# A new instruction order from planned times, and six more spinning products in the opening

## The chip, the cores and the metric

The kernel runs on one core of one Trainium2 chip. The metric is device time in microseconds (us) for one execution of the whole program. Beside the timed runs there is one execution under the hardware profiler, and all the lines quoted come from that one. The engines are TensorE (PE, with its weight loads shown as PEld), VectorE (DVE), ScalarE (ACT), GpSimd (POOL) and SyncE (SP). Each runs its own instructions in order, and they wait for each other through semaphores.

## What is computed

A sequence of 2048 rows of 512 passes twice through a pair of blocks, A and B, each added to its input after a layer norm.

```python
def _A_ref(x, mem0, Wq, Wk, Wv, Wo, seg_len):        # 32 heads of 128, 8 memory rows, segments of 32
    for s in range(n_seg):
        xs = x[:, s * seg_len:(s + 1) * seg_len, :].copy()
        h = jnp.concatenate([mem, xs], axis=1)
        q, k, v = (einsum('btd,dhe->bhte', h, W) for W in (Wq, Wk, Wv))
        scores = jnp.where(mask, einsum('bhqe,bhke->bhqk', q, k) * scale, -1e9)
        o = einsum('bhqk,bhke->bhqe', softmax(scores), v)
        o = einsum('bhte,hed->btd', o, Wo)
        mem = o[:, :M, :].copy()
        outs.append(o[:, M:, :])
...
x = x + _A_ref(_layernorm(x), A_mem0, A_Wq, A_Wk, A_Wv, A_Wo, A_seg_len)
x = x + _B_ref(_layernorm(x), B_wqkv, B_wo)          # linear attention, 32 heads of 16
x = x + _A_ref(_layernorm(x), A_mem0, A_Wq, A_Wk, A_Wv, A_Wo, A_seg_len)
x = x + _B_ref(_layernorm(x), B_wqkv, B_wo)
```

What matters is the loop in A: 64 segments a layer, and the first eight rows of a segment's output are the memory rows that the next segment begins with. So the segments form one long chain, and everything else has to be fitted around it.

## The kernel before

All of Wq, Wk, Wv and Wo lie in SBUF (16 MB, loaded once in the opening, 1 MB or half a MB at a time). A segment's 40 columns (8 memory rows, 32 rows of x) are handled in two parts: the memory rows with the first 24 rows of each segment go through the segment's own steps, while the last 8 rows of four segments are gathered into a "left" block of 32, which is projected ahead of time. The eight heads of a quarter sit in four column strips of the PE array, so nearly every product is a group of four matmuls with 32 columns of weights each, side by side. A product over 512 inputs is four such groups, one a quarter of the weight matrix (c = 0 to 3), summed in one of eight PSUM banks.

One segment of the chain, by the names of its nodes and the lines of its matmuls:

- `kq0`, `kq1`: key and query products of the two halves of the heads (L2282, and L2139 where the weights are already loaded), copied out (L2009 on ACT or L2010 on DVE) and transposed on DVE (L2301);
- `v`: value products;
- `mem0`, `mem1`: for each half the scores (L2434 and L2426), their exponentials (L2441, L2445), a mask (L2449) and the product with the values for the memory rows (L2462), then a reciprocal, a scaling and a transpose (L2467 to L2469);
- `out`: eight groups of the output product (L2554), copied out;
- `next`: the new memory rows, turned into columns by two small products (L2584) and copied into the next segment's block;
- `x`: attention of the other rows (L2504, L2524), which nothing in the chain waits for;
- `left0`, `left1`, `leftv`, `prep`, `res`, `bi`, `bo`, `bl`: left blocks, layer norms, residuals, and the steps of block B, which are woven in.

No loop sets the order. Each operation is a node with a key (layer, step, name) and a count within it. A table, `PLACE`, holds one number for each node; `schedule` sorts all nodes by it, and each engine issues its own in that order. A letter behind the number chooses the engine of a copy that either can do: `a` for ACT, `v` for DVE. Another table, `BANKS`, gives the PSUM bank of each product. In this version the numbers are ranks, of 13,822 nodes:

```python
    (0, 39, "next"): "4257 4258 4262a",
    (0, 40, "kq0"): "4265 4269 4271 4273 4281a 4289 4277a 4285",
```

`finalize` turns the dependencies into semaphore waits. Where a node has more than one, all but the one expected last may be moved to an earlier instruction of the same engine that waits for nothing, if the producer is expected to be done by then. The expectation is made of ranks: the producer's rank plus 60 for a DMA, or plus 2 and 9 times its cost.

In the opening the weights arrive over the queue of SP: four quarters of Wk, four of Wq, four of Wv, eight pieces of Wo. PE meanwhile projects the keys and queries of left blocks 0 to 6 (`sk` and `sq`, two halves each), those of blocks 3 to 6 being written to HBM (`spill`, on POOL, after the last piece of Wo) and read back later (`lre`, on SP). Before there is anything to do, PE "spins": `spin` multiplies a tile of ones by itself, three groups of four 256-column matmuls for each spin (L2167). There are eight spins, and every first key or query product is ordered behind the last of them.

## Time and profile before

| | us |
|---|---|
| median of three runs | 1471.38 |
| lowest and highest | 1468.09, 1471.46 |
| the profiled execution | 1467.64 |
| its span, first to last instruction | 1465.6 |

The profile's page gives busy time by engine, the chain of waits that ended last, and groups of instructions by line. In a group's row stand the output and input, the shape, the count, the busy time, the mean length of one in ns, and the idle time of the engine just before with what ended it. In a timeline's row stand the start and the length in us, then engine, line and operation; an "x" counts instructions merged into the row. Lengths of matmuls include the pipeline's drain, so two rows can overlap; the distance between two starts tells how fast PE really goes. The granted clock of the profile is 1.00 throughout.

### The profile page before, as it was taken

Reading aid. Unit: us, or ns where it says so; the run is one execution under the profiler, and the core shown is the slowest. Engines: PE = TensorE matmul, PEld = TensorE weight load, DVE = VectorE, ACT = ScalarE, POOL = GpSimd, SP = SyncE. Lnnn points to the kernel's source line nnn. Section 1 sums busy time; section 2 is a strip of 40 time slices with the busy share of each in tenths; the row PEclk is TensorE's granted clock in tenths of the full one; section 3 lists DMA queues with packets and bytes.
Section 4 is the critical chain, followed back from the end, with each engine's and each line's share of the span. In section 5 each row is a group of like instructions: output and inputs, shape, how many; then the busy total and the mean of one; then the engine's idle time right before and its main releaser. Section 6 shows DMA issues by size and latency. Waiting matters only on the chain.

```text
span 1465.6 us, 90842 instructions
## 1 busy us (share of the span) xinstructions
PE 1440.9 (98%) x43565; PEld 830.5 (57%) x39581; DVE 1222.8 (83%) x3879; ACT 922.6 (63%) x2620; POOL 205.4 (14%) x407
## 2 busy tenths in 40 slices
PE   8999999999999999999999999999999999999998
PEld 4455655655555555555455555556565555655555
DVE  4788888888888888988888888888788888888878
ACT  4656566666656666565566666656766766666657
POOL 3111111011111101111201110111111011111010
PEclk9999999999999999999999999999999999999999
DMA  9421111111011011002300101111001011101034
GB/s 386 151 72 43 18 51 37 31 22 29 22 21 21 19 24 25 25 22 46 75 21 21 26 21 28 25 27 28 22 22 28 24 29 25 29 18 25 28 65 129
DMA packets 84967, 65.12 MB, mean 44 GB/s; under 512 B 65544, under 2 KB 76360, under 8 KB 83048
## 3 DMA queue, kind: packets, MB, share of 16 engines
q1 hardware_dynamic: 70584, 40.21, 10.4%
q0 software_dynamic: 13840, 18.98, 4.5%
q8 instruction: 325, 5.32, 1.5%
q14 instruction: 58, 0.48, 0.1%
q10 hardware_dynamic: 160, 0.14, 0.0%
HBM read 27.80 MB, written 14.02 MB: 29 GB/s over the span
## 4 chain that ended last, share of the span: by engine, by line
PE 93%; DVE 4%; DMA 2%; ACT 1%; issue 1%; SPq 0%; DVEq 0%
PE pb L2282 43%; PE pb L2554 19%; PE pb L2139 14%; PE pb L2504 3%; PE pb L2151 3%; PE pb L2741 2%; PE pb L2462 2%; PE pb L2524 2%; PE pb L2426 2%; PE pb L2584 1%; DMA Wk_sb<-in_A_Wk_dram 1%; DVE arena_sb L2010 1%; PE pb L2434 1%; DVE arena_sb L2301 0%; DMA arena_sb<-xn_scratch 0%
## 5 line engine op out<-in xcount | busy, mean ns | idle before, releaser
L2009 ACT ACTIVATE arena_sb<-pb 128x512 bf16<-128x512 f32 (+3 forms) x1036 | 515.1, 527 | 245.8 <-PE pb L2139 107.7
L2282 PE MATMUL pb<-Wk_sb,arena_sb 128*32 128x512 bf16 x4320 | 357.3, 382 | 3.8 <-DMA Wk_sb<-in_A_Wk_dram 1.5
L2282 PE MATMUL pb<-Wv_sb,arena_sb 128*32 128x512 bf16 x4608 | 328.7, 378 | 0.0
L2554 PE MATMUL pb<-Wo_sb,arena_sb 128*32 128x256 bf16 x10368 | 322.7, 273 | 3.3 <-issue 2.4
L2301 DVE STREAM_TRANSPOSE arena_sb<-arena_sb 128x256 f32<-128x256 f32 x640 | 259.5, 425 | 38.4 <-ACT arena_sb L2009 31.2
L2554 PEld LDWEIGHTS pb<-Wo_sb,arena_sb 128*32 128x32 bf16 x10368 | 265.9, 97 | 40.3 <-DVE arena_sb L2469 8.7
L2026 POOL DMA_DIRECT2D dx_sb<-y_sb x246 | 125.5, 514 | 1008.0 <-DVE y_sb L2566 369.8
L2282 PE MATMUL pb<-Wq_sb,arena_sb 128*32 128x512 bf16 x3088 | 235.4, 379 | 0.1
L2282 PEld LDWEIGHTS pb<-Wk_sb,arena_sb 128*32 128x32 bf16 x4320 | 117.4, 97 | 193.9 <-issue 91.1
L2477 ACT ACTIVATE arena_sb<-pb,arena_sb 128x128 bf16<-128x128 f32 x539 | 163.5, 368 | 66.7 <-DVE arena_sb L2511 33.5
L2139 PE MATMUL pb<-Wq_sb,arena_sb 128*32 128x512 bf16 x2032 | 199.4, 379 | 0.0
L2479 DVE TENSOR_TENSOR arena_sb<-pb,arena_sb 128x128 bf16<-128x128 f32 (+2 forms) x391 | 157.1, 402 | 9.0
L2282 PEld LDWEIGHTS pb<-Wv_sb,arena_sb 128*32 128x32 bf16 x4608 | 113.1, 96 | 80.5 <-issue 8.5
L2010 DVE CAST arena_sb<-pb 128x512 bf16<-128x512 f32 (+2 forms) x226 | 112.0, 500 | 40.6 <-PE pb L2139 12.2
L2009 ACT ACTIVATE outW_sb<-pb 128x256 f32<-128x256 f32 (+1 forms) x132 | 50.5, 383 | 139.0 <-PE pb L2554 90.5
L2282 PEld LDWEIGHTS pb<-Wq_sb,arena_sb 128*32 128x32 bf16 x3088 | 82.9, 97 | 87.8 <-issue 21.2
L2514 DVE STREAM_TRANSPOSE arena_sb<-arena_sb 128x192 f32<-128x192 f32 x256 | 93.5, 365 | 19.3 <-ACT arena_sb L2477 16.7
L2492 DVE TENSOR_TENSOR arena_sb<-arena_sb,wx_sb 128x1280 bf16<-128x1280 bf16 x128 | 102.0, 797 | 1.8 <-ACT arena_sb L2445 1.1
L2504 PE MATMUL pb<-arena_sb 128*32 128x130 bf16 x3072 | 102.4, 220 | 0.9 <-issue 0.8
L2449 DVE TENSOR_TENSOR arena_sb<-arena_sb 128x256 bf16<-128x256 bf16 x252 | 70.1, 280 | 22.5 <-ACT arena_sb L2441 19.5
L2504 PEld LDWEIGHTS pb<-arena_sb 128*32 128x32 bf16 x3072 | 67.7, 96 | 30.3 <-issue 9.2
L2566 DVE TENSOR_TENSOR y_sb<-pb,outW_sb 64x256 bf16<-64x256 f32 x162 | 68.7, 424 | 16.4 <-ACT outW_sb L2009 11.1
(135 smaller groups left out, 1793.9 us busy)
## 6 DMA issues: line engine op xcount, KB each, us to landing
Wk_sb<-in_A_Wk_dram SPq DMA_DIRECT2D x4, 1024.0 KB, 10.7
Wq_sb<-in_A_Wq_dram SPq DMA_DIRECT2D x4, 1024.0 KB, 17.4
Wv_sb<-in_A_Wv_dram SPq DMA_DIRECT2D x4, 1024.0 KB, 25.3
Wo_sb<-in_A_Wo_dram SPq DMA_DIRECT2D x8, 512.0 KB, 22.1
xs_scratch<-x_sb POOLq DMA_DIRECT2D x32, 128.0 KB, 2.5
pq_scratch<-arena_sb POOLq DMA_DIRECT2D x23, 128.0 KB, 2.6
xn_scratch<-arena_sb POOLq DMA_DIRECT2D x20, 128.0 KB, 2.8
lk_scratch<-arena_sb POOLq DMA_DIRECT2D x8, 256.0 KB, 4.1
```

The source lines that it names most:

```text
L2009: return e.activation(o() if callable(o) else o, i() if callable(i) else i, ACTF.Copy)
L2010: return e.tensor_copy(o() if callable(o) else o, i() if callable(i) else i)
L2026: add(eng, lambda e: e.dma_start(o, i), 0.55 if eng == "pool" else 0.66, reads=reads, writes=writes, dsem="%s%d" % (kind, k), lat=lat + (0 ...
L2139: return pe.add_instruction(mybir.InstMatmult(name=nc.get_next_instruction_name(), engine=mybir.EngineType.PE, ins=[pe.lower_ap(x), pe.low ...
L2282: r = pe.matmul(o, blk[:, c, :], w, start=(c == 0), stop=(c == 3), tile_position=(0, 32 * j))
L2301: add("dve", lambda v: v.transpose(dst, src(img[:, k, :].bitcast(F32))), 0.445, reads=[("img", k, h) for h in range(2)], writes=[dkey])
L2477: x = e.activation(o[:, u, :], i()[:, u, :], ACTF.Copy, scale=r[:, u:u + 1])
L2479: return e.tensor_tensor(o, i(), r.unsqueeze(2).to_broadcast([128, n, 128]), ALU.mult)
L2492: add("dve", lambda v: v.tensor_tensor(Px.rearrange("p b (n j x) -> p b n j x", n=20, j=4), PQx[:, r2].rearrange("p b (n x) -> p b n x", n ...
L2504: r = pe.matmul(pv.f32()[32 * i:32 * i + 32, 130 * k:130 * k + 130], cols(b, k, i), vimg[:, r2, 4 * b + i, :], start=True, stop=True, skip ...
L2514: add("dve", lambda v, b=b, k0=k0: v.transpose(oTb[:, s1, b, :, :, k0:k0 + 3].rearrange("p h j k q e -> p k (h j) (q e)").bitcast(F32), ox ...
L2554: r = pe.matmul(tl.f32()[32 * j:32 * j + 32, 0:256], oT[:, b, f, n, :, :, e], Wo_sb[:, 16 * b + 4 * n + 2 * f + e, 256 * d:256 * d + 256], ...
```

## The change

The table `PLACE` is replaced as a whole, and so is `BANKS`. The nodes and their keys are the same apart from nine more spins. The new numbers are planned times in ns instead of ranks. The same two lines, with those they are read with in the prediction, old and then new:

```diff
-    (0, 39, "next"): "4257 4258 4262a",
-    (0, 39, "x"): "4242 4251 4252 4256 4266 4268v 4283 4294 4295 4296 4304 4313v 4331 4253 4254 4263 4279v 4302",
-    (0, 40, "kq0"): "4265 4269 4271 4273 4281a 4289 4277a 4285",
-    (0, 42, "left1"): "4231 4235 4249 4259 4272v 4275 4333a 4342",
+    (0, 39, "next"): "444451 444529 444870a",
+    (0, 39, "x"): "442488 443680 443850 444607 445022 445225v 445810 443736 443793 444664 446090 446283v 450524 443906 449926 450271 450452a 451109",
+    (0, 40, "kq0"): "445152 445584 446016 446448 447202v 447920 447111a 448260",
+    (0, 42, "left1"): "444020 444721 450935 451367 455086v 455805 456272a 456901",
```

The opening's spins, first products and reads, old and then new:

```diff
-    (0, -3, "spin"): "13 17 18 21 24 28 46 65",
-    (0, 0, "kq0"): "61 79 119 124 229 233 234 240 239a 244 276a 282",
-    (0, 4, "sk"): "82 83 108 122 129a 133",
+    (0, -3, "spin"): "2904 3232 3559 3886 4214 4542 6201 6529 7614 7942 8713",
+    (0, -2, "spin"): "10719 11046 11374 11701 12029 12356",
+    (0, 0, "kq0"): "9208 17551 18198 20898 35788 36004 37299 37515 37222a 37861 38813a 40853",
+    (0, 4, "sk"): "9640 14414 16903 19596 20255a 20885",
```

The expectation in `finalize` is now the producer's planned time, plus its latency and 200 ns for a DMA, or its cost and 100 ns (300 on PE):

```diff
-        place = {nd: i for i, nd in enumerate(self.committed)}
         source = {}
         for nd in self.committed:
             if nd.dsem is not None:
-                source[sidx[nd.dsem], nd.dval] = place[nd] + 60
+                source[sidx[nd.dsem], nd.dval] = nd.t + 1000 * nd.lat + 200
             elif nd.sig:
-                source[sidx[nd.eng], nd.val] = place[nd] + 2 + 9 * nd.cost[nd.eng]
+                source[sidx[nd.eng], nd.val] = nd.t + 1000 * nd.cost[nd.eng] + (300 if nd.eng == "pe" else 100)
...
-                        if source[w] >= place[o]:
+                        if source[w] > o.t:
```

The opening has eleven spins instead of eight ahead of the first products, and six more behind the products of the first quarter of Wk: `lead` holds the first groups of blocks 0 and 2 (both halves) and of 4 and 5 (one half). With the first group of `kq0`, which `hold` puts ahead of the six as well, these make seven groups. The other three groups of `kq0`'s key product and of all the others come behind the last of the six:

```diff
-            last = spin(0, -3, "spin", 8, fresh=3)
+            last = spin(0, -3, "spin", 11, fresh=3)
             early[0] = True
+            lead, rest = [], []
...
-                        for n in P.nodes[n0:]:
-                            if n.engs == ("pe",):
-                                n.order.update(last)
+                        mine = [n for n in P.nodes[n0:] if n.engs == ("pe",)]
+                        mine[0].order.update(last)
+                        if not u and G in (0, 2, 4, 5) and not (G > 2 and b):
+                            lead.append(mine[0])
+                        rest += mine[1:]
+            n0 = len(P.nodes)
+            last = spin(0, -2, "spin", 6, after=lead)
+            for n in rest:
+                n.order.update(last)
+            hold.extend([P.nodes[n0], last[0]])
...
+                    if not b:
+                        hold[0].order.add(P.nodes[n0])
+                        for n in P.nodes[n0 + 1:n0 + 4]:
+                            n.order.add(hold[1])
```

The reads of spilled keys and queries have four semaphores instead of two:

```diff
-                        writes=[(nm, G % 2, b) for b in range(2)], dsem="dlr%d" % u, lat=3.5)
+                        writes=[(nm, G % 2, b) for b in range(2)], dsem="dlr%d" % (2 * (G % 2) + u), lat=3.5)
```

More of the change, by code (lines that the diff above doesn't have):

```diff
@@ L1598 @@
[L1598 to L1602 removed]
+    "5012300000002233403606556732127530265702617371111110143430427612101762547164571615674120565271153721"
@@ new lines @@
+    "5327354723537241374215432547015731472453172531512433701572432472670637427362432136472317243172363045"
+    "4105473612764724356123442516212556106712760122162601673210732076750551362765170231701234057641206421"
+    "0675432132431024715647542657121434012762512471564716457213645162560211307026107260270651240736420635"
+    "1600274206537043601604325160532405320457752354730052053725012730123746023017546374015214052714625071"
+    "2521732746630215602657037061307314073176010570410735106472064672650134524365421425537621056324523436"
@@ L1603 @@
+    "0047054136572140704125760034163231666357511357301273063046275163520761247501753067257435745703417504"
+    "3146635461316224254650036601253360146213402536154221042763415724015273174603763037703626421453412531"
+    "5137061046310463075065741765703540613460514726437141475731744322145273270766611046523023710461420054"
+    "4233422775401633735115"
 )
@@ L2305, in a_layer @@
         early = [False]
+        hold = []
         def lroom(G):
@@ L2688, in a_layer @@
                 if b or first and s == 0:
+                    n0 = len(P.nodes)
                     tk, tq = [project(blk, bk, p)[0] for p in parts]
+                    if not b:
+                        hold[0].order.add(P.nodes[n0])
+                        for n in P.nodes[n0 + 1:n0 + 4]:
+                            n.order.add(hold[1])
                 else:
```

40 lines of the change are left out of this document (15 added, 25 removed), and 3100 rows, old and new, of the table PLACE.

## The prediction

> **What bounds the kernel now.** I read the page's head and its chain of waits first, then the busy times by stage, then the timeline of the stretches where TensorE (PE) is not full, and last the two tables of the diff, node by node.
>
> ```profile
> span 1465.6 us, 90842 instructions
> PE 1440.9 (98%) x43565; PEld 830.5 (57%) x39581; DVE 1222.8 (83%) x3879; ACT 922.6 (63%) x2620; POOL 205.4 (14%) x407
> PE 93%; DVE 4%; DMA 2%; ACT 1%; issue 1%; SPq 0%; DVEq 0%
> ```
> ```profile
> 100.00:650.00 550.00, 547.62 (x16886) 319.00 (x15292) 467.96 (x1541) 343.30 (x1008) 77.39 (x148) 1.00 0.12 28
> 650.00:750.00 100.00, 94.23 (x2687) 50.83 (x2456) 83.84 (x250) 56.89 (x150) 18.31 (x33) 1.00 0.23 53
> 750.00:1400.00 650.00, 647.75 (x19956) 374.68 (x17968) 549.85 (x1756) 427.04 (x1232) 85.05 (x163) 1.00 0.10 24
> 1400.00:1466.00 66.00, 58.14 (x1688) 35.57 (x1616) 54.01 (x133) 43.19 (x93) 3.20 (x6) 0.99 0.43 104
> ```
> PE sets the end: 93% of the chain, 98% busy. The columns of the second fence are the stretch, PE, weight loads, DVE, ACT, POOL, clock, DMA. No other engine is full, and no stage is bound by DMA after the opening. But "busy" hides something. A matmul's record ends after its drain, so the records overlap, and a pause of about 0.1 us between two of them shows as no idle time at all. Here is one place in the first layer and one in the second:
>
> ```profile
> 452.31 0.23 PE L2504 MATMUL pb<-arena_sb 128*32 128x130 bf16 x4
> 452.36 0.29 PE L2584 MATMUL pb<-selm_sb,outW_sb 128*32 128x16 f32 x16
> 452.48 0.39 PE L2282 MATMUL pb<-Wq_sb,arena_sb 128*32 128x512 bf16 x4
> 452.70 0.39 PE L2139 MATMUL pb<-Wk_sb,arena_sb 128*32 128x512 bf16 x4
> 453.02 0.40 PE L2282 MATMUL pb<-Wk_sb,arena_sb 128*32 128x512 bf16 x4
> ```
> ```profile
> 1339.48 0.28 PE L2584 MATMUL pb<-selm_sb,outW_sb 128*32 128x16 f32 x16
> 1339.60 0.60 PE L2151 MATMUL pb<-arena_sb 128*32 128x512 bf16 x8
> 1339.89 0.19 DVE L2010 CAST arena_sb<-pb 128x32 bf16<-128x32 f32 x1 [0.16 <-PE pb L2584]
> 1340.14 0.40 PE L2282 MATMUL pb<-Wk_sb,arena_sb 128*32 128x512 bf16 x4
> ```
> Read starts, not lengths. L2584 makes the next memory rows; they are copied out (L2010 here), and only then can the next segment's key and query product (L2282) begin. In between PE has one filler: two groups of four 512-column matmuls, each 0.22 us after the other (452.48 to 452.70). The second group is issued by 452.92, yet the next product starts at 453.02. In the other place 1339.60 + 0.43 = 1340.03, and the product starts at 1340.14. From the last L2584 to the product the hand-over needs about 0.54 us, and the filler covers 0.43. So 0.1 us is lost, unseen in the idle column.
>
> I did this for every PE node: start to start, less the lower quartile of that step among nodes of the same shape. These undisturbed steps add up to 1392.6 us for the whole program, so no order can win more than 1465.6 - 1392.6 = 73 us. Of that, 49 us lie between 100 and 1400 us. By hand-over, over the whole program:
>
> - memory rows to the first product of the next segment: 14.7 us, over 126 hand-overs of which 107 pause (the two places above are of these);
> - second half's scores to its memory product (L2426 to L2462): 5.7 us; first half's: 3.5 us;
> - output product to memory rows (L2554 to L2584): 4.4 us; first memory product to output product (L2462 to L2554): 4.0 us;
> - products to scores, and the second memory product to the output product: 1.7 us together.
>
> **The change part by part.** *The new table.* All operations stay; only their order on each engine changes, and the engine of some copies. A gain can come only from more work standing in these hand-overs. In both tables I added the undisturbed steps of the PE nodes that stand between the two ends, and took the need from the hand-overs that pause now. The shortfall is need less cover, summed.
>
> *Memory rows to next product.* Segment 39 of layer 0 is the place at 452 us. Its old ranks put one filler after "next" (left1, 4259, before kq0 at 4265). The new times put two L2504 groups (x, 444607 and 444664), then left1 (444721), then kq0 (445152). An L2504 group before "next" costs 0.05 us (452.31 to 452.36), 0.056 as quartile, so the cover goes from 0.43 to 0.54. Over all 126 the mean cover goes from 0.43 to 0.52 us; covers under 0.52 fall from 111 to 43. With needs of 0.543 (copy on ACT) and 0.538 (on DVE) the shortfall falls from 15.5 to 5.9. Scaled to the measured 14.7 that leaves 5.6: **-9.1 us**. The groups put there stood elsewhere, so the other hand-overs must be counted too.
>
> *Scores to memory product.* First half: mean cover 1.40 to 1.53 us, shortfall at a need of 1.17 from 5.6 to 0.9, so 3.5 becomes 0.6: **-2.9**. Second half: 1.27 to 1.31, at 1.28 from 14.2 to 11.5, so 5.7 becomes 4.6: **-1.1**.
>
> *Given back.* First memory product to output: 1.31 to 1.25, at 1.13 from 8.5 to 10.6: **+1.0**. Output to memory rows: 0.70 to 0.68, at 0.66 from 3.8 to 4.5: **+0.8**. Second memory product to output: **+0.1**. Second half's products to scores: 1.61 to 1.52: **+0.4**. First half's products to scores: 2.39 to 2.17 us, the largest cut. Only two of these pause today (need about 2.0), and the quickest takes 1.51, so the shortfall grows by 0.3 us (need 1.5) to 4.9 (need 2.0). I take 1.8, a need that lies between: **+1.8**.
>
> *Copies.* 404 move from ACT to DVE and 355 back. DVE gets 49 more:
>
> ```profile
> L2010 DVE CAST arena_sb<-pb 128x512 bf16<-128x512 f32 (+2 forms) x226 | 112.0, 500 | 40.6 <-PE pb L2139 12.2 <-PE pb L2584 8.3 <-PE pb L2504 8.1
> L2009 ACT ACTIVATE arena_sb<-pb 128x512 bf16<-128x512 f32 (+3 forms) x1036 | 515.1, 527 | 245.8 <-PE pb L2139 107.7 <-PE pb L2282 44.9 <-PE pb L2584 31.1
> ```
> At 500 ns, 49 copies bring DVE from 1222.8 to about 1247 us, 85% of the span. Its idle time shrinks by a tenth, and if the pauses left in the middle (about 39 us) grew alike, it would cost 4 us. They wait on other engines too: I take **+1.0**, bounds 0 and 4.
>
> *The opening.*
>
> ```profile
> 2.16 4.03 PE L2167 MATMUL pb<-one_sb 128*32 128x256 bf16 x72 [2.16 <-POOL one_sb L2083]
> 7.44 0.62 PE L2207 MATMUL pb<-id_sb,arena_sb 128*32 128x128 bf16 x16 [0.51 <-DVE arena_sb L2196]
> 7.84 0.86 PE L2167 MATMUL pb<-one_sb 128*32 128x256 bf16 x12
> 9.22 0.62 PE L2282 MATMUL pb<-Wk_sb,arena_sb 128*32 128x512 bf16 x4
> 9.62 0.86 PE L2167 MATMUL pb<-one_sb 128*32 128x256 bf16 x12
> 12.00 0.62 PE L2282 MATMUL pb<-Wk_sb,arena_sb 128*32 128x512 bf16 x4 [1.52 <-DMA Wk_sb<-in_A_Wk_dram]
> ```
> ```profile
> 12.00:14.80 2.80, 2.80 (x28) 1.11 (x32) 0.80 (x3) 0.00 (x0) 2.26 (x8) 1.00 1.00 424
> 14.80:16.90 2.10, 2.10 (x44) 1.03 (x40) 0.00 (x0) 0.00 (x0) 1.59 (x7) 1.00 1.02 429
> ```
> Today PE does one first-quarter product at 9.22, one spin, and waits for the second quarter of Wk until 12.00. It then runs at half speed: 28 matmuls, or 7 groups, in 2.80 us, against 0.22 us a group from 14.8 on. By 16.9 some 18 groups are done. A spin is three groups of four 256-column matmuls, 4.03/6 or some 0.65 us at half speed and 0.33 at full. The new order puts three more spins ahead of the first product, then seven first-quarter products, then six spins, and only then the second quarter. If the three close the hole before 7.44 and the clock has risen by about 9.5, the seven end near 11, the spins near 13, and by 16.9 all 24 groups are done that eight PSUM banks allow with three quarters landed: six groups, 1.3 us ahead. If the clock rises only at 14.8 as today, the first product slips to 10.6 (three spins of 0.65 less the 0.51 idle), the seven end at 13.6, the spins at 16.2, and by 16.9 only 10 groups are done: eight, 1.7 us, behind. The wait that six spins add holds all PE work behind them; nothing else on PE is ready meanwhile, apart from what the second quarter frees at 12.0.
>
> [...]
>
> What is won early meets the last piece of Wo:
>
> ```profile
> L2045 SPq DMA_DIRECT2D Wo_sb<-in_A_Wo_dram x8: 439/2130/6250, 12.1 to 29.7; - x8
> DMA to landing us min/median/max: 18.1/22.1/26.0
> 47.73 1.93 PE L2554 MATMUL pb<-Wo_sb,arena_sb 128*32 128x256 bf16 x64 [0.18 <-DVE arena_sb L2469]
> 48.99 3.76 POOL L2363 DMA_DIRECT2D lk_scratch<-arena_sb  x7 [32.23 <-DMA Wo_sb<-in_A_Wo_dram]
> ```
> It is issued at 29.7 and lands no earlier than 47.8 (shortest flight 18.1) and no later than 48.99, when POOL, which waited for it, goes on. The first output's seventh product, which reads it, comes at 47.73 + 6 x 0.22 = 49.05. So at most 1.25 us and at least 0.06 of a lead survive. I take **-0.5**; bounds -1.25 and +1.7.
>
> *The rest.* The rule that moves a second wait to an earlier instruction now goes by planned times. It changes where an engine stops, not when the producer ends: 0, bounds -1 and +1. The reloads of spilled keys get four semaphores for two; they land many microseconds early: 0. Layer switch and end (650 to 750 and past 1400) lose 5.8 and 7.9 us of PE today; both are reordered, and their waits are on chains of DVE and ACT that stay: 0, bounds -4 and +3.
>
> Sum: -9.1 - 2.9 - 1.1 + 1.0 + 0.8 + 0.1 + 0.4 + 1.8 + 1.0 - 0.5 = -8.5 us. The profiled execution took 1467.6 (span 1465.6 and 2.0 around it), so its like would take 1459.1. The median of the runs, 1471.4, lies 3.7 higher; from it the forecast is **1462.9 us**.
>
> **The rivals.** *The pauses only move.* If a segment is bound by its chain rather than by PE work, cover put into one hand-over is missed in the next: 1471, no change. For it: the same groups are moved. Against it: PE pauses some 49 us over 1300, so per segment it is almost all work, and most hand-overs on the chain do not pause.
>
> *Slower: products to scores.* The one place where the order takes away 0.22 us of cover is L2282 to the first scores (L2434), on a path of two copies and two DVE transposes. If the fuller DVE lifts its need from below 1.9 to 2.5, the shortfall grows by 17.0 us in place of my 1.8: 1462.9 + 15.2 = 1478. At a need of 2.3 (12.2 us) the time is 1473, so it decides from there. Against it: with covers of 1.89 today almost none pauses.
>
> *The clock opens no earlier than today* and six spins at half speed stand in the way: +1.7 for -0.5, so 1465.1; it doesn't change the sign.
>
> *More comes out of it.* The layer switch and the end win their 4 us, and the second half's scores win what the first do (5.7 to 1 us, 3.6 more): 1455.
>
> **How the numbers follow.** A measurement tells about 0.3% (4.4 us) from no change: faster is below 1467.0, slower above 1475.8. Forecast, with its own scatter of 5 us, 0.55; more 0.14; late clock 0.05; pauses only move 0.17; slower 0.09. Of the forecast and the late clock some 0.05 fall within 0.3%, and of the moved pauses 0.05 fall outside, 0.03 of them faster: faster 0.72, same 0.17, slower 0.11. The range 1455 to 1474 holds the forecast, the case of more, and no change.
>
> **What would show it.** In the new timeline two L2504 groups stand between L2584 and L2282 and the product starts right after its filler, with no 0.1 us hole; the 126 pauses add to about 6 us. The first scores start within 0.05 us after the matmul ahead of them. In the opening the seven groups end before 11.5 and 512-column groups go at 0.22 us from 13 on; the first output product waits for Wo. I am wrong if these holes stay, or if L2434 or L2462 opens new ones of 0.1 us in most segments.

## The result, and the profile after

The changed kernel takes 1475.11 us (median of 11 runs, 1471.41 to 1479.71), the kernel before in the same series 1469.98 (11 runs, 1467.17 to 1472.04). The ratio is 1.0036, with an interval of 1.0022 to 1.0050: slower, though by little, where 1462.9 us and a range of 1455 to 1474 were forecast.

The first lines of the page of the changed kernel, and its chain of waits:

```profile
span 1472.8 us, 90913 instructions
...
PE 1434.8 (97%) x43673; PEld 839.5 (57%) x39641; DVE 1244.9 (85%) x3928; ACT 897.7 (61%) x2532; POOL 205.6 (14%) x407
...
PE 86%; DVE 5%; DMA 5%; ACT 1%; SPq 1%; issue 1%; POOL 1%; DVEq 0%
PE pb L2282 39%; PE pb L2563 18%; PE pb L2139 13%; PE pb L2151 3%; PE pb L2513 3%; DMA dx_sb<-y_sb 2%; PE pb L2755 2%; PE pb L2471 2%; PE pb L2533 2%; PE pb L2435 2%; PE pb L2593 1%; DMA arena_sb<-arena_sb 1%; DVE arena_sb L2488 1%; DMA x_s
```

PE fell from 93% of the chain to 86%, DMA rose from 2% to 5%, and a transfer that takes 3.0 us of the chain in the kernel before takes 36.5 us of it here, 2.5% of the span: `dx_sb<-y_sb`. These are the eight small transfers of a residual (L2026, `res`, counts 12 to 19), which bring a block's output rows into the layout of x, four each from the queues of SP and POOL. Only the residual's add (L2633 before, L2642 after) uses them.

The stages of the changed kernel, with the columns of the prediction's second fence (the last 6.8 us of the span are left out):

```profile
100.00:650.00 550.00, 538.23 (x16680) 315.59 (x15108) 467.31 (x1522) 333.28 (x976) 75.28 (x144) 0.99 0.12 26
650.00:750.00 100.00, 94.80 (x2748) 53.39 (x2532) 84.39 (x249) 61.41 (x161) 19.34 (x35) 1.00 0.24 54
750.00:1400.00 650.00, 644.71 (x19904) 380.08 (x17912) 561.53 (x1792) 406.24 (x1162) 83.00 (x159) 1.00 0.10 25
1400.00:1466.00 66.00, 59.50 (x1788) 35.10 (x1708) 56.56 (x144) 45.38 (x104) 6.27 (x12) 1.00 0.38 88
```

In the first layer PE now has 11.8 us without work where it had 2.4, in the second 5.3 where it had 2.3. So this time the loss shows as idle time. What PE and DVE waited for says where. First DVE's waits for the residual's transfers, in us, times and longest, in the kernel before:

```profile
DVE x_sb L2633 <- DMA dx_sb<-y_sb: 3.2, 2, 2.3
DVE arena_sb L2531 <- DMA dx_sb<-y_sb: 0.8, 1, 0.8
```

The same view of the changed kernel, its six costliest rows:

```profile
DVE arena_sb L2523 <- DMA dx_sb<-y_sb: 5.6, 4, 2.8
DVE arena_sb L2010 <- DMA dx_sb<-y_sb: 3.6, 4, 2.4
DVE arena_sb L2842 <- DMA dx_sb<-y_sb: 2.7, 2, 1.7
DVE arena_sb L2301 <- DMA dx_sb<-y_sb: 2.4, 2, 1.4
DVE x_sb L2642 <- DMA dx_sb<-y_sb: 1.8, 1, 1.8
DVE arena_sb L2488 <- DMA dx_sb<-y_sb: 1.7, 1, 1.7
```

17.8 us in 14 stops (20.0 in 17 with two smaller rows), for 4.0 in 3. L2523 and L2301 are transposes, L2010 a copy, L2488 a product, L2842 a step of block B: none of these five reads `dx_sb`. The waits were put on them by `finalize`. And PE's waits in the changed kernel, the two costliest rows:

```profile
PE pb L2443 <- DVE arena_sb L2301: 8.5, 5, 2.4
PE pb L2471 <- DVE arena_sb L2458: 4.8, 3, 1.7
```

They are the first scores behind the transposes, and the memory product behind the mask: the chain, behind a DVE that stands still. The same two rows of the kernel before:

```profile
PE pb L2434 <- DVE arena_sb L2301: 0.5, 1, 0.5
PE pb L2462 <- DVE arena_sb L2449: 0.2, 1, 0.2
```

One place of the first layer shows it whole (timeline of the changed kernel; some rows left out):

```profile
213.65 1.00 POOL L2026 DMA_DIRECT2D dx_sb<-y_sb  x2
...
213.91 0.43 DVE L2301 STREAM_TRANSPOSE arena_sb<-arena_sb 128x256 f32<-128x256 f32 x1
213.93 1.41 SPq L2026 DMA_DIRECT2D dx_sb<-y_sb  x2
...
216.76 0.23 DVE L2010 COPY arena_sb<-arena_sb 128x256 bf16<-128x256 bf16 x1 [2.42 <-DMA dx_sb<-y_sb]
216.90 0.76 DVE L2301 STREAM_TRANSPOSE arena_sb<-arena_sb 128x256 f32<-128x256 f32 x2
...
217.40 0.21 PE L2443 MATMUL pb<-arena_sb 128*32 128x64 bf16 x4 [2.01 <-DVE arena_sb L2301]
```

The copy at 216.76 belongs to a left block (`ql` of segment 17). It carries the wait for the four transfers of SP for the residual of step 16, and DVE, ready for it at 213.91 + 0.43 = 214.34, stood for 2.42 us. The transposes of the keys behind it waited too, and with them PE. The add that needs the data runs at 222.30, 5.5 us later.

Why was the wait put there? One semaphore counts the four transfers, 16 for each, and the program numbers them as it makes the nodes: counts 13, 15, 17 and 19 get 208, 224, 240 and 256. `finalize` takes the planned time of the one that bears the number waited for, 256: 209.919 us, with 2.0 of latency and the 200 ns 212.119, ahead of the copy's 212.310. But the plan issues that transfer first. The one numbered 208 is planned last, at 212.799, and 256 is reached only when all four have landed, by the plan's own times at 214.8, 2.49 us behind the copy. SP's row in the same trace:

```profile
211.87 3.47 SPq L2026 DMA_DIRECT2D dx_sb<-y_sb  x5
```

These five are the four and another small transfer of `res` (count 1), which stands fourth; the starts in the trace are 211.87, 212.58, 213.26, 213.93 and 214.71. The wait ended 2.05 us after the last of them: the plan's latency is right, its transfer is the wrong one. So counted, 13 of the changed kernel's 226 moved DMA waits stand up to 2.5 us ahead of their planned landing, 15.7 us in sum. In the kernel before the same mistake stands in the code, but 60 ranks, some 6.4 us (1465.6 us by 13,822 nodes, times 60), cover the spread of the four; in the change 2.2 us do not.

Nothing behind the copy ran on DVE in the 2.42 us, though the transposes' inputs had no part in the wait.

What the prediction looked for is there too. The hand-over from segment 39 to 40, in the changed kernel:

```profile
455.00 0.29 PE L2593 MATMUL pb<-selm_sb,outW_sb 128*32 128x16 f32 x16
455.12 0.29 PE L2513 MATMUL pb<-arena_sb 128*32 128x130 bf16 x8
455.24 0.40 PE L2282 MATMUL pb<-Wq_sb,arena_sb 128*32 128x512 bf16 x4
455.45 0.40 PE L2139 MATMUL pb<-Wk_sb,arena_sb 128*32 128x512 bf16 x4
455.67 0.40 PE L2282 MATMUL pb<-Wk_sb,arena_sb 128*32 128x512 bf16 x4
455.88 0.40 PE L2139 MATMUL pb<-Wq_sb,arena_sb 128*32 128x512 bf16 x4
```

Two L2513 groups (the old L2504) and a left block's filler stand before the key product, and it starts at 455.67, 0.22 us behind the filler's last group: no hole. It happens at 455.67 instead of 453.02, though.

### The profile page after: what moved, and what is told of

Its sections match the earlier page's. It is cut to its first block, busy times and chain, and to the rows that moved or that the text cites. A ratio compares the mean times of both kernels' runs of the same rounds, so it can differ in the third digit from the quotient of the medians.

```text
span 1472.8 us, 90913 instructions
## 1 busy us (share of the span) xinstructions
PE 1434.8 (97%) x43673; PEld 839.5 (57%) x39641; DVE 1244.9 (85%) x3928; ACT 897.7 (61%) x2532; POOL 205.6 (14%) x407
## 3 DMA queue, kind: packets, MB, share of 16 engines
q1 hardware_dynamic: 70584, 40.21, 10.2%
q8 instruction: 326, 5.34, 1.6%
## 4 chain that ended last, share of the span: by engine, by line
PE 86%; DVE 5%; DMA 5%; ACT 1%; SPq 1%; issue 1%; POOL 1%; DVEq 0%
PE pb L2282 39%; PE pb L2563 18%; PE pb L2139 13%; PE pb L2151 3%; PE pb L2513 3%; DMA dx_sb<-y_sb 2%; PE pb L2755 2%; PE pb L2471 2%; PE pb L2533 2%; PE pb L2435 2%; PE pb L2593 1%; DMA arena_sb<-arena_sb 1%; DVE arena_sb L2488 1%; DMA x_sb<-in_A_x_dram 1%; SPq L2026 1%
## 5 line engine op out<-in xcount | busy, mean ns | idle before, releaser
L2009 ACT ACTIVATE arena_sb<-pb 128x512 bf16<-128x512 f32 (+3 forms) x1013 | 501.4, 524 | 257.5 <-PE pb L2139 108.2
L2282 PE MATMUL pb<-Wv_sb,arena_sb 128*32 128x512 bf16 x4608 | 332.6, 380 | 0.0
L2301 DVE STREAM_TRANSPOSE arena_sb<-arena_sb 128x256 f32<-128x256 f32 x640 | 259.7, 427 | 35.4 <-ACT arena_sb L2009 25.7
L2026 POOL DMA_DIRECT2D dx_sb<-y_sb x246 | 125.2, 513 | 997.6 <-DVE y_sb L2575 459.3
L2282 PE MATMUL pb<-Wq_sb,arena_sb 128*32 128x512 bf16 x3088 | 238.0, 380 | 1.1 <-DVE arena_sb L2010 1.1
L2282 PEld LDWEIGHTS pb<-Wk_sb,arena_sb 128*32 128x32 bf16 x4320 | 122.8, 96 | 176.0 <-issue 87.4
L2139 PE MATMUL pb<-Wq_sb,arena_sb 128*32 128x512 bf16 x2032 | 201.4, 379 | 0.0
L2486 ACT ACTIVATE arena_sb<-pb,arena_sb 128x128 bf16<-128x128 f32 x469 | 142.9, 369 | 72.5 <-DVE arena_sb L2540 22.7
L2488 DVE TENSOR_TENSOR arena_sb<-pb,arena_sb 128x128 bf16<-128x128 f32 (+2 forms) x422 | 171.3, 406 | 11.5 <-DMA dx_sb<-y_sb 1.7
L2010 DVE CAST arena_sb<-pb 128x512 bf16<-128x512 f32 (+2 forms) x248 | 127.4, 516 | 30.9 <-PE pb L2282 8.3
L2282 PEld LDWEIGHTS pb<-Wq_sb,arena_sb 128*32 128x32 bf16 x3088 | 86.0, 97 | 88.1 <-issue 26.3
L2513 PE MATMUL pb<-arena_sb 128*32 128x130 bf16 x3072 | 106.7, 219 | 0.2
L2523 DVE STREAM_TRANSPOSE arena_sb<-arena_sb 128x192 f32<-128x192 f32 x256 | 93.4, 365 | 15.1 <-ACT arena_sb L2486 6.6
L2471 PEld LDWEIGHTS pb<-arena_sb 128*32 128x32 bf16 x2016 | 45.5, 96 | 72.0 <-ACT arena_sb L2009 33.9
L2513 PEld LDWEIGHTS pb<-arena_sb 128*32 128x32 bf16 x3072 | 69.2, 96 | 29.8 <-issue 6.5
```

The source lines that it names most:

```text
L2009: return e.activation(o() if callable(o) else o, i() if callable(i) else i, ACTF.Copy)
L2010: return e.tensor_copy(o() if callable(o) else o, i() if callable(i) else i)
L2026: add(eng, lambda e: e.dma_start(o, i), 0.55 if eng == "pool" else 0.66, reads=reads, writes=writes, dsem="%s%d" % (kind, k), lat=lat + (0 ...
L2139: return pe.add_instruction(mybir.InstMatmult(name=nc.get_next_instruction_name(), engine=mybir.EngineType.PE, ins=[pe.lower_ap(x), pe.low ...
L2282: r = pe.matmul(o, blk[:, c, :], w, start=(c == 0), stop=(c == 3), tile_position=(0, 32 * j))
L2301: add("dve", lambda v: v.transpose(dst, src(img[:, k, :].bitcast(F32))), 0.445, reads=[("img", k, h) for h in range(2)], writes=[dkey])
```

## The experiments

All are compared with the kernel before, run on the same chip in the same series: 1469.42 us for the first four, 1469.51 for the next four, 1467.32 for the three after, 1469.57 for the run after these, 1470.74 for the last two. Ratios have their interval in brackets. "Moved" counts the DMA waits that DVE holds on an instruction other than the one that needs them, from the kernel's own lists; "closest" is the planned time from the transfer to the nearest of them.

**The old expectation on the new order.** The changed kernel, but `finalize` counts in ranks as before:

```diff
-                source[sidx[nd.dsem], nd.dval] = nd.t + 1000 * nd.lat + 200
+                source[sidx[nd.dsem], nd.dval] = place[nd] + 60
...
-                        if source[w] > o.t:
+                        if source[w] >= place[o]:
```

(and the engines' expectation likewise).

> The changed kernel's order, with the old rule for moving a second wait (producer's rank plus 60 for a DMA). Theory A, the moved DMA waits: DVE stops for dx_sb DMAs fall from 20 us to about 4, and the time to 1459 to 1465, faster than before. Theory B, the new order or the fuller DVE is itself slower: the time stays at 1472 to 1478.

1454.53 us, 0.9895 [0.9882, 0.9907]: 149 moved, none closer than 4.9 us. The time lies below theory A's range (1459 to 1465). So the new order, with its engines, banks, opening and four semaphores, wins some 15 us under the old rule, and the new rule takes away some 20. DVE's waits for the transfers fall to the residual's own:

```profile
DVE x_sb L2643 <- DMA dx_sb<-y_sb: 1.7, 3, 0.6
```

**Early waits on the old order.** The kernel before with 25 ranks for a DMA instead of 60:

```diff
-                source[sidx[nd.dsem], nd.dval] = place[nd] + 60
+                source[sidx[nd.dsem], nd.dval] = place[nd] + 25
```

> The kernel before, with one number changed: a DMA is expected 25 ranks after its issue instead of 60 (25 ranks at 106 ns are 2.65 us, what the new rule takes). Theory A: more DMA waits are moved ahead on DVE, its stops for dx_sb DMAs grow from 4 us to 12 or more, and the time is 4 to 15 us above before. Theory B: within 2 us of before.

1480.97 us, 1.0082 [1.0068, 1.0097]: 219 moved instead of 129, the nearest 26 nodes behind its transfer instead of 61. Its costliest rows:

```profile
DVE arena_sb L2010 <- DMA dx_sb<-y_sb: 3.1, 3, 1.6
DVE arena_sb L2514 <- DMA dx_sb<-y_sb: 3.1, 4, 1.0
DVE x_sb L2633 <- DMA dx_sb<-y_sb: 2.5, 3, 1.2
DVE arena_sb L2727 <- DMA dx_sb<-y_sb: 2.4, 1, 2.4
```

The same stops, at the same kinds of instruction, without anything of the new order: 11.6 us.

**No wait moved**, and **a later landing**. Two edits of the changed kernel, each alone:

```diff
-                if e in ("sp", "pool") or nd.key[:2] < (0, 0):
-                    continue
+                continue
```
```diff
-                source[sidx[nd.dsem], nd.dval] = nd.t + 1000 * nd.lat + 200
+                source[sidx[nd.dsem], nd.dval] = nd.t + 1000 * nd.lat + 4200
```

> The changed kernel with no wait moved at all: every wait stays with the instruction that needs it. Theory A: no DVE stop of over 1 us for dx_sb except at the residual's own addition, and 1459 to 1468; what it lies above the run with the old rule is what moving is worth. Theory B: 1472 or more.

> The changed kernel with its rule by planned times, but 4 us more for a DMA. Theory A: like the old rule, 1459 to 1465; if the planned times of the other engines were at fault instead of the DMAs' it would stay near 1475. Theory B: 1472 or more.

Without moves 1462.07 us, 0.9944 [0.9932, 0.9956], in theory A's range. With 4200 ns 1453.59, 0.9895 [0.9880, 0.9909], again below it: 141 moved, none closer than 6.25 us, and this one number is the whole edit. DVE's waits for the transfers in the second:

```profile
DVE x_sb L2642 <- DMA dx_sb<-y_sb: 2.4, 1, 2.4
```

That settles that moved waits made the change slower, but not yet which and why; the first of the last pair of runs below does. It leaves another question: why no move at all costs 8.5 us more than late moves. I first took it for the price of waits left where they are needed. Then PE's waits in the kernel without moves showed something else:

```profile
PE pb L2150 <- issue: 3.2, 2, 2.4
PE pb L2166 <- POOL one_sb L2082: 2.2, 1, 2.2
PE pb L2562 <- issue: 2.1, 5, 0.7
PE pb L2470 <- DVE arena_sb L2487: 1.8, 4, 0.6
PE pb L2206 <- DVE arena_sb L2195: 1.7, 4, 1.0
PE pb L2512 <- issue: 1.6, 3, 1.1
```

"Issue" means that the engine waited for nothing that the profile shows. Summed over all rows these stops take 9.0 us, and 3.1 with the late landing, which is 5.9 of the 8.5.

**The opening's spins**, each group alone, on the kernel with 4200 ns. Without the six later ones (and the orders that hang on them), and without three of the eleven first:

```diff
-            last = spin(0, -2, "spin", 6, after=lead)
-            for n in rest:
-                n.order.update(last)
-            hold.extend([P.nodes[n0], last[0]])
+            for i in range(6):
+                P.tile()
```
```diff
             tl = P.tile()
+            if step == -3 and i in (6, 7, 10):
+                P.count += 1
+                continue
```

> The new order with the DMA margin of 4200 ns (1453.6 us), without the six later spins; the eleven first ones stay. In the new trace 512-column groups already run at 0.22 us each from 9.1 us, before the six, and PE's clock opens at about 6.6 us, when the second pair of spins closes a hole of 0.8 us. Theory (the three extra first spins open the clock, the six do nothing): 1452.5 to 1454.5 us, and the first output product starts as early as before, near 46 us. Rival (the six keep the clock open while PE waits for the second quarter of Wk): groups of 0.43 us return behind 11 us, the first output product starts 1 to 2 us later, 1454.6 to 1456 us.

> The same kernel (1453.6 us) with the six later spins but without three of the eleven first ones: the two at about 6.7 us and the one at 8.8 us. Theory (closing the hole at 6.7 us opens the clock): groups of 0.43 us return at 9.1 us, the first output product starts 1 to 2 us later and 1454.6 to 1456 us are taken. Rival (the prediction's: a lead in the opening meets the last piece of Wo and is worth 0.5 us at most): 1453.6 to 1454.1 us.

1462.52 us, 0.9958 [0.9942, 0.9974], and 1461.06, 0.9954 [0.9939, 0.9969]. Both lie above either theory's range. The opening did not get longer. The seventh product of the first output, the one that needs the last of Wo, starts at 46.47 and 46.84 us, 47.80 with all spins. The time goes later, in issue stops: 10.9 and 10.4 us for 3.1. So neither theory of the opening told anything of these times, and the experiment that seemed to be about spins became one about issue stops.

**The old order with a wide margin** (150 ranks instead of 60), and **the changed kernel with 1700 ns**:

> The old order with a margin of 150 ranks for a DMA in place of 60: DVE's moved DMA waits fall from 129 to 25, all at least 156 nodes behind their DMA, and 103 more waits stay on their own DVE instruction. Theory (the new order itself is worth about 15 us, and early waits cost the old one little): 1466 to 1471 us, with no stop of DVE for the residual's inputs outside the residual, so 12 us or more above the new order with a safe margin (1453.6). Rival (the order is worth the 8.5 us of the sum, and the rest of the 15 comes from stops that the old order also has): 1461 to 1463 us.

> The changed kernel with 1700 ns in place of 200 behind a DMA's latency: 196 moved DMA waits on DVE (226 with 200, 141 with 4200), the closest planned 3.74 us behind its DMA (2.21 with 200, 6.25 with 4200). Theory (each wait that stands ahead of the real landing stops DVE): the stops that need less than 3.7 us go, those of queued transfers stay; 4 to 10 us of stops, 1456 to 1465 us. Rival (only the closest waits do the harm): 1453 to 1455 us. Rival (it isn't the distance but the number of moved waits): 1467 to 1470 us, as 196 of 226 stay moved.

The first: 1469.90 us, 1.0008 [0.9997, 1.0019], 25 moved. The order's rival fell: the old order has nothing to win from later waits, the 15 us belong to the new one. The second: 1455.90 us, 0.9911 [0.9897, 0.9925], with 196 moved, none closer than 3.74 us. It lies between the theory's range (from 1456, with 4 to 10 us of stops) and that of the rival that blamed the closest alone (up to 1455); the rival is the nearer, since DVE's stops for these transfers were 2.5 us in all, and PE's issue stops 6.2 us for 3.1. The third, which counted the moved waits alone, fell. The costliest of DVE's rows is the residual's own:

```profile
DVE x_sb L2642 <- DMA dx_sb<-y_sb: 1.8, 4, 1.1
```

So the harm comes from among the waits that this margin no longer moves (30 fewer in sum) or moves less far: 19 us (1475.1 - 1455.9).

**No DMA wait moved**, engines' waits moved as in the change:

```diff
-                        if source[w] > o.t:
+                        if source[w] > o.t or names[w[0]] in dsems:
```

> The changed kernel with every DMA wait left on its own instruction; waits for engines are still moved. DVE keeps 313 second waits (172 with the margin of 4200 ns, 324 with no wait moved at all), PE 192 (178 and 368). Measured so far: 1453.6 us with the margin, 1462.1 with no wait moved, but PE's stops that wait for nothing ("issue" in the waits) are 3.1 us in the first and 9.0 in the second. Theory (moving a wait in time is worth little; most of the 8.5 us are issue stops): PE's waits for DVE, ACT and DMA stay within 2 us of those with the margin (11.6 us), and the time is 1450.5 to 1452.5 us plus this run's issue stops. Rival (a second wait left on DVE costs time): the waits for DVE grow by 3 us or more, whatever the issue stops.

1453.87 us, 0.9911 [0.9897, 0.9924], issue stops 2.5: 1453 to 1455 had been expected from these. PE's waits for DVE are 9.2 us as with the late landing, though DVE holds 313 second waits for 172. So a second wait on DVE costs nothing that can be seen here, and moving DMA waits, which cost the change 20 us, had some 2 us to win as far as this pair tells (0.9895 against 0.9911, with intervals that overlap).

**Where the issue stops come from.** Three edits of the later spins, on the kernel with 4200 ns: five instead of six; the sixth of twice the length (12 matmuls more); and one with three weight loads of its own instead of six:

```diff
-            last = spin(0, -2, "spin", 6, after=lead)
+            last = spin(0, -2, "spin", 1, after=lead, fresh=3)
+            for i in range(5):
+                P.tile()
```

> The kernel with the margin of 4200 ns (1453.6 us) with five spins behind the first quarter of Wk in place of six: 12 matmuls fewer among 43,700, all in the first 13 us. Without all six the time was 1462.5 us, and PE's issue stops rose from 3.1 to 10.9 us, at places from 207 to 1438 us, each ending 1.2 to 1.6 us after a 16 KB packet of the queue that brings PE's instructions. Theory (what counts is where the packets' borders fall in the program): the issue stops change again, anywhere between 2 and 11 us, the waits for other engines stay within 2 us, and the time is 1450.5 to 1452.5 us plus the issue stops. Rival (the spins themselves win the time): 1453 to 1455.5 us, with issue stops of 2.5 to 4.5 us.

> The same kernel (1453.6 us) with a sixth spin of twice the length: 12 matmuls more. Theory (the packets' borders): 1450.5 to 1452.5 us plus this run's issue stops, which may be anything between 2 and 11 us. Rival (the spins themselves win the time): 1453 to 1455 us, with issue stops of 2 to 4 us.

> The kernel with the margin of 4200 ns (1453.6 us, 0.9895 of the kernel before) with one spin of three weight loads behind the first quarter of Wk in place of six: PE then has 72 instructions fewer (weight loads counted), as many fewer as in the run without three of the first spins, where the issue stops were 10.4 us. Against the kernel with the margin, PE's instructions were 72 and 96 fewer in the two runs without spins and 182 more in the one with no wait moved, the three with 9 to 11 us of issue stops; a 16 KB packet holds 256 instructions of 64 bytes, and counted round in 256 these are shifts of 184, 160 and 182. The runs with shifts of -16 to +14 had 2.5 to 6.2 us. Theory (the packets' borders): 9 to 12 us of issue stops, near 252, 1412 and 1430 us as in that run, 1459 to 1463 us (0.994 to 0.997). Rival (those three runs had their stops for reasons of their own): 2.5 to 5 us, 1452 to 1456 us.

| | PE instructions against 4200 ns | counted round in 256 | issue stops, us | ratio |
|---|---|---|---|---|
| 4200 ns | 0 | 0 | 3.1 | 0.9895 |
| 1700 ns | 0 | 0 | 6.2 | 0.9911 |
| old expectation | -10 | 246 | 4.5 | 0.9895 |
| five spins | -16 | 240 | 3.9 | 0.9896 |
| sixth spin twice as long | +12 | 12 | 3.9 | 0.9915 |
| no DMA wait moved | +14 | 14 | 2.5 | 0.9911 |
| without six spins | -96 | 160 | 10.9 | 0.9958 |
| without three first spins | -72 | 184 | 10.4 | 0.9954 |
| one spin with three loads | -72 | 184 | 10.3 | 0.9951 |
| no wait moved | +182 | 182 | 9.0 | 0.9944 |

The times were 1451.94, 1454.77 and 1460.88 us. The first two runs told nothing apart: both theories had allowed such issue stops (and the time of five spins lies below either range, in a series in which the kernel before took 2 us less, too). The third did. Its first lines and those of the kernel with 4200 ns give the count, 60 matmuls and 12 weight loads fewer:

```profile
PE 1430.5 (98%) x43613; PEld 844.9 (58%) x39629; DVE 1244.9 (85%) x3928; ACT 896.7 (61%) x2532; POOL 205.1 (14%) x407
```
```profile
PE 1428.7 (98%) x43673; PEld 838.8 (58%) x39641; DVE 1244.9 (86%) x3928; ACT 895.6 (62%) x2532; POOL 204.8 (14%) x407
```

With a shift of -72 by other means than in the run without three first spins, the issue stops came back, and the longest at the same place. The timeline of the run without three first spins, then of the run with one spin:

```profile
1433.48 1.83 PE L2151 MATMUL pb<-arena_sb 128*32 128x128 bf16 x29 [2.83 <-issue]
```
```profile
1433.57 1.99 PE L2151 MATMUL pb<-arena_sb 128*32 128x128 bf16 x29 [2.83 <-issue]
```

Another came at 1412.1 us for 1411.7. At the third named place, 252 us, 0.35 us came back of 0.83, and a stop at 210 us had grown from 0.38 to 1.06 us.

**The right transfer.** The changed kernel with its 200 ns and its planned times, and the landing taken from the last of all transfers up to the value; then the same on the old order with 25 ranks:

```diff
-                source[sidx[nd.dsem], nd.dval] = nd.t + 1000 * nd.lat + 200
+                source[sidx[nd.dsem], nd.dval] = max(
+                    o.t + 1000 * o.lat for o in self.committed if o.dsem == nd.dsem and o.dval <= nd.dval) + 200
```
```diff
-                source[sidx[nd.dsem], nd.dval] = place[nd] + 25
+                source[sidx[nd.dsem], nd.dval] = max(
+                    place[o] for o in self.committed if o.dsem == nd.dsem and o.dval <= nd.dval) + 25
```

> The changed kernel, 200 ns and planned times kept, but a DMA's semaphore value counts as reached when the last of all transfers up to that value is expected, not the one that bears the number. Numbers are given as the program makes the nodes, and the plan issues a residual's four transfers of a queue in another order: in the trace at 211 to 217 us five transfers leave SP, at 211.87, 212.58, 213.26, 213.93 and 214.71; by the plan the one numbered last (256) is the first, the one numbered 208 the last, and the wait for 256 ends at 216.76, 2.05 us after the last. By the plan's own times 13 of the 226 moved waits of the changed kernel then stand up to 2.5 us ahead of their landing, 15.7 us in sum. With the edit 215 stay moved, none ahead of its landing. Theory (the 13 waits on the wrong transfer are the whole harm; the 200 ns are enough): 1452 to 1456.5 us (0.988 to 0.9915), DVE's waits for the residual's transfers 4 us or less, on the add itself. Rival (200 ns are too little, since the run leaves the plan by microseconds): 1458 to 1472 us, with stops of DVE on other instructions left.

> The kernel before with 25 ranks for a DMA, which took 1481.0 us, with the same correction: the rank of the last of all transfers up to the value. 213 waits are moved instead of 219 (129 with 60 ranks); the nearest stands 26 nodes behind the last transfer, where it stood one node ahead of it. Theory (the wrong transfer): most of the 11.6 us go, 1468 to 1473 us (0.999 to 1.0025). Rival (25 ranks, some 2.6 us, are too little for any transfer): 1476 to 1482 us.

The first: 1457.89 us, 0.9906 [0.9890, 0.9923], with 215 waits moved. The ratio is within the theory's, the time 1.4 us above it, in a series in which the kernel before took 1.3 us more than beside the 4200 ns. This correction, with eleven moved waits fewer in sum, takes away 17 of the 20 us. DVE's waits for the transfers that are left:

```profile
DVE x_sb L2643 <- DMA dx_sb<-y_sb: 3.2, 4, 2.2
DVE arena_sb L2489 <- DMA dx_sb<-y_sb: 1.1, 1, 1.1
DVE arena_sb L2011 <- DMA dx_sb<-y_sb: 0.4, 1, 0.4
DVE arena_sb L2524 <- DMA dx_sb<-y_sb: 0.3, 1, 0.3
```

5.0 us, where 4 had been the bound: 3.2 on the add itself, and 1.8 in three stops elsewhere. So the 200 ns are a little short as well, but that is the small part.

The second: 1477.53 us, 1.0044 [1.0030, 1.0058]. It is in the rival's range, and the theory fell for the old order, as put: the correction takes away 0.4% of the 0.8%. The stops of DVE on instructions that need no `dx_sb` fell from 12.0 to 5.7 us, yet the issue stops rose from 5.3 to 8.8 with as many instructions, and 25 ranks stay a short distance. How these share what is left was not taken apart.

## Why the prediction was wrong

**The step that failed** is the sentence on the rule that moves a second wait: "It changes where an engine stops, not when the producer ends: 0, bounds -1 and +1." The first half is true, and there lies the cost: where an in-order engine stops decides what stands behind it (the 2.42 us at the copy held the transposes, and PE for 2.01). I asked neither how far behind its transfer a wait now stands nor which transfer the rule looks at. Both stand in the diff's lines and the table: by the plan's own times 13 waits are too early, by 15.7 us in sum. Measured it is +20 us (1475.11 against 1454.53 and 1453.59), of which 17 go when only the transfer is corrected. No rival had it. The sign that the prediction named for being wrong did show, new holes before L2434 and L2462 (now L2443 and L2471), though in a few long stops and not in most segments.

**The table was sized too small.** -8.5 was forecast; with the waits out of the way it was 1454.5, 14.9 us under the kernel before, or 12.5 by the profiled spans (1453.1 for 1465.6). PE's pauses, counted start to start as in the prediction (recounted with the same steps for all kernels, which moves the column of before by up to 0.3), in us:

| hand-over | before | after | old expectation | 4200 ns | forecast | measured with old expectation |
|---|---|---|---|---|---|---|
| memory rows to next product | 14.7 | 6.1 | 6.2 | 6.4 | -9.1 | -8.5 |
| first scores to memory product | 3.4 | 4.7 | 0.8 | 0.7 | -2.9 | -2.6 |
| second scores to memory product | 5.5 | 11.2 | 6.5 | 7.1 | -1.1 | +1.1 |
| first memory product to output | 3.7 | 3.5 | 3.3 | 3.2 | +1.0 | -0.5 |
| output to memory rows | 4.4 | 3.8 | 3.9 | 3.5 | +0.8 | -0.6 |
| second memory product to output | 0.4 | 0.8 | 1.1 | 0.6 | +0.1 | +0.7 |
| second half's products to scores | 1.5 | 6.3 | 1.2 | 1.2 | +0.4 | -0.3 |
| first half's products to scores | 1.2 | 6.7 | 1.7 | 1.6 | +1.8 | +0.5 |
| all pauses | 71.5 | 75.7 | 55.7 | 54.9 | | -15.8 |

The two big terms were right in mechanism and size. The terms given back were mostly not due: +4.1 in sum, -0.2 measured. A likely reason, which no run shows: the needs were assumed, and a need set too high makes losses of hand-overs that still fit. The second scores' term had the wrong sign. The eight rows win 10.1 us together; the other 5.7 of the 15.8 lie in pauses outside these rows, for which the prediction had -0.5 (the opening) and 0, and were not taken apart. Against all pauses, -15.8, the nine more spins count as work, some 3.0 us at 0.33, which brings it near the 12.5 of the spans.

The after column is read against the one with 4200 ns: 20.8 us more, of which 10.2 at the products to scores, some 4 at each of the two memory products, and the rest elsewhere. The order's gain at the memory rows is untouched.

**Fuller DVE, +1.0:** DVE's busy time rose to 1244.9 as reckoned (1247), and PE's waits for DVE with the old expectation are 9.2 us for 7.7 before. That agrees, though it is not shown to be the copies.

**The opening, -0.5.** The size fits and most of its reasons don't. The seventh product of the first output, due at 49.05 us in the profile of before, starts at 47.65, 47.43 and 47.09 in the three other kernels with the old opening, and at 46.5 to 48.4 in the twelve with a new one; the means are 47.8 and 47.6. So most of the lead that one profile of each shows is scatter. The bound on Wo was too hard: the last piece landed at 46.6 us in the changed kernel, not 47.8 at the earliest. And PE's rate does not go by the spins alone. The spin at 7.7 us and the first products behind the second quarter, in two kernels with the old opening, first that with 25 ranks, then that with 150:

```profile
7.69 0.50 PE L2167 MATMUL pb<-one_sb 128*32 128x256 bf16 x12
...
10.20 2.77 PE L2282 MATMUL pb<-Wk_sb,arena_sb 128*32 128x512 bf16 x48 [0.62 <-DMA Wk_sb<-in_A_Wk_dram]
```
```profile
7.85 0.85 PE L2167 MATMUL pb<-one_sb 128*32 128x256 bf16 x12
...
10.45 3.44 PE L2282 MATMUL pb<-Wk_sb,arena_sb 128*32 128x512 bf16 x49 [0.21 <-DMA Wk_sb<-in_A_Wk_dram]
```

With the same matmuls in the same order, the first runs at the faster rate from about 6.3 us (12 matmuls in 0.50), the second only from about 11 (0.85, and 49 matmuls of 512 columns in 3.44 us for 48 in 2.77), the profiled kernel before from 14.8, and the fourth with the old opening from 6.6. In the twelve kernels with a new opening the rate rose at 4.7 to 8.1 us, without three of the first spins at 6.9. So these three are not needed for an early rise; whether the new opening as a whole spares the late rises, which two of four kernels with the old one had, so few traces can't tell. That the rise comes early in most runs, on which the -0.5 rests, no run shows; what they show in its place is the two means, 0.2 us apart.

The traces' records of the granted clock begin, with 1.00, at 14.67 us in the kernel before and at 6.12 in the changed kernel, there ahead of the second pair of spins (6.54); for the time before, where the views print 1.00, there is none. Later the changed kernel has three stretches of 3.41 us at 0.50, from 217.75, 473.75 and 838.97 us, at the three stops of PE of over 2 us (2.01, 2.35 and 2.05, which end at 217.40, 474.01 and 838.57); at its other stops behind 6.12, of up to 1.73 us, the record stays at 1.00. Why the rise comes late in some openings no run shows.

**The rest.** Layer switch and end lie within 1 us of before in the kernel with the old expectation, as forecast (0). The reloads' four semaphores were not tried alone. "The pauses only move" is refuted by 1454.5 us. "Slower: products to scores" named the place where half of the loss showed (1.2 to 6.7 us and 1.5 to 6.3), but not for its reason: with the same covers and the waits further back the two stay at 1.6 and 1.2.

## What to carry to other kernels

Before a wait is moved ahead on an in-order engine, ask when the semaphore reaches its value: with several transfers on one semaphore that is when all of them have landed (here 2.05 us after the last of them started), whichever bears the number, and reckoning with the wrong one of four cost more here (17 us) than a new order of 13,800 operations had won (15). Read what an engine waited for by producer, and ask of each row whether that instruction uses the data at all. And where an edit changes the number of instructions, look at the stops that wait for nothing before giving its few microseconds to its purpose.

## What the runs showed of the hardware

PE's stops in which it waits for nothing fall together with the packets of one DMA queue. It stands on the page of the changed kernel as:

```profile
q8 instruction: 326, 5.34, 1.6%
```

326 packets with 5.34 MB, 16 KB each; for 83,491 instructions of PE (43,673 matmuls, 39,641 weight loads, 177 waits) that is 64 bytes each, 256 to a packet (326.1 packets; the kernel before, with 325, has 83,329, which by the same count are 325.5). That the queue brings PE's instructions is an estimate from these counts. In the sixteen traces PE stopped 71 times for over 0.7 us between two matmuls or weight loads of one line, waiting for nothing; each of the 71 stops ended 1.21 to 1.58 us after the end of one such packet, which come 4.5 us apart on average (1472.8 by 326). Of 172 such stops that did wait for a semaphore, only 23 ended that long after one. The two longest of all, from the trace's list of packets:

```
stop at us   length us   PE goes on after a packet's end by us
1430.4       3.05        1.32      (without three first spins)
1430.5       3.05        1.55      (one spin with three loads)
```

The sum of PE's issue stops was 2.5 to 6.2 us in eleven of the sixteen kernels profiled. In the new order it was 9.0 to 10.9 in just the four whose instruction count lay 160 to 184 off, round in 256, and only the run with one spin was built to test that. The count alone does not settle it: the two kernels of the old order with 25 ranks have as many instructions and 5.3 and 8.8 us. That PE stands there for a late packet is an estimate too, from those distances; why it does at some borders and not at others stays open.
